# Linear attention and two mixtures of experts on one core: fewer and moved filler products, two transfers' first chunk ahead, and a reordered end of the attention

## The chip, the cores and the metric

The kernel runs on one core of a Trainium2 chip. The metric is device time of one execution in microseconds. The kernel before takes 455.93 us (median of 3 runs, 455.37 to 456.27).

## The reference

Three layers in a row, all in fp32. First a gated linear attention over 2 batches, 8 heads, 768 positions and a head width of 48; its output is the 1536 x 384 matrix x of the two layers behind it. Then a mixture of experts with one expert for each token, then one with two experts for each token and noise on the gate:

```python
for t in range(S):                                                  # attention
    state = alpha[:, :, t, :, None] * state + einsum('bhd,bhe->bhde', k[:, :, t], v[:, :, t])
    y[:, :, t] = einsum('bhd,bhde->bhe', q[:, :, t], state)
...
logits = x @ w_gate; expert_idx = argmax(logits)                    # layer 1: 8 experts, F = 1024
y = einsum('ecf,efd->ecd', maximum(einsum('ecd,edf->ecf', disp, w1), 0), w2)
...
noisy = x @ w_gate + log1p(exp(x @ w_noise)) * noise                # layer 2: the best two of 8
out[mask] += top2_w[mask, k] * (maximum(x[mask] @ w1[e], 0) @ w2[e])
```

## The kernel before

**Attention.** The 1536 positions are cut into 12 chunks of 128, numbered 0 to 11 (6 for each batch). They come into the core in five transfers, `PIECES`: (0,0), (0,2) and (0,4) with two chunks each, (1,0) and (1,3) with three; the numbers are the batch and its first chunk. (0,0) is worked on as two parts of one chunk. For each transfer `decays` (L217) makes running products of alpha on VectorE with scans (L253 to L269) and multiplies k and q by them (`times`, L243 and L244). Each of k and q has two halves in time, so there are four such multiplications for a transfer; the last two (L273, L275) complete k and q. `decays` is a generator, and each `yield` is a place where other work may be put between.

A chunk i goes through four steps. `scores` (L295): TensorE transposes k (L303), multiplies k by q (L309), ScalarE copies the results out of PSUM (L305, L317) and GpSimd zeroes the upper triangle (`affine_select`, L318). `state` (L322): the running state (L334, L336), scaled by ScalarE or VectorE (L341, L343). `mix` (L348): the output of the chunk (L356, L360, L362), copied out by ScalarE (L365). `r1_logits` (L378): the output is turned to rows and the gate's logits come with it in one product (L385); VectorE sums the logits (`gates`, L387) and ScalarE copies the rows (L394). Both read the same PSUM tile, and the one that the program names second waits for the other. `gates` comes second except for the last chunk (L390, L395).

**Routing.** Chunks are routed in groups (`GROUPS`: 0 to 2, 3 to 5, 6 and 7, 8 and 9, 10, 11). `route1` (L404) is a generator of eight steps: maximum, index and difference, one-hot row (L420), exponential on ScalarE (L422), ranks by products of ones with the one-hot rows on TensorE (L426 to L430), normalising (L432 to L435), slot numbers (L440 to L447), and the scatter of the rows to DRAM by GpSimd's indirect DMA (L158). Rows of chunks 8 to 11 (`EARLY`) aren't read back for the first expert: `first_x` (L649) takes the first 240 rows of that expert from DRAM by three transposing products (L655) and adds the four late chunks by products with one-hot columns (L662).

**Order.** The order around the change is written out by hand. `PATTERNS` has a string for each chunk i; its letters are S (`scores` of chunk i+1), T (`state`), M (`mix`), L (`r1_logits` of chunk i-1), D (a step of `decays`), R (a step of the oldest route) and W (`splits`: a piece of expert 0's weights is rounded to fp32r by ScalarE, L537, and the rest that is left goes to VectorE or GpSimd, L538). `FXR` orders what comes behind chunk 11: x is a step of `first_x`, l the logits of chunk 11, R as above. Each engine works through its own instructions in that order.

**Fillers.** `warm(n)` (L167) issues n products of a zero tile (128x512, bf16, L170) whose result nobody reads: 34 (`WARM0`) ahead of the first `scores`, 10 (`WARM2`) ahead of that of chunk 1, 20 (`FILL`) ahead of that of chunk 2, and 2 (`WARM1`) in `first_x`.

**Experts.** Behind the attention 16 experts follow (8 of each layer), each with `hidden` (L683, L686) and `second` (L714, L716 or L722), each fp32 product made of three fp32r ones. Weights come by DMA from SP's queue and are split as above. At the end the last rows go to the output by indirect DMA.

Of the kernel before, what the change touches and what calls it, by code (L numbers as in the profile page):

```python
# [12 lines left out]
ALU = mybir.AluOpType  # L13
# [17 lines left out]
P1 = C1 // T1  # L31
R = N
SPARE = E * R
WARM0 = 34
NF, ND = F // 128, DM // 128
IW = HR + E
PIECES = [(0, 0, 2), (0, 2, 2), (0, 4, 2), (1, 0, 3), (1, 3, 3)]
# [2 lines left out]
MASKS = "G" * 12  # L40
STATES = "AAAAAAAAVVVV"
DECAYS = "444444440000"
FILL = (20,)
S0 = 1
WARM1 = 2
WARM2 = 10
FXR = "xRRxRRlxRRRRRxxRxRR"
EARLY = 8
WE = "GGGGVVVVVVVVVGGG"
PATTERNS = (  # L50
    "SDDTDDM", "SDDTLDDM", "SDDTLDDM", "SDDTLRRRDDM", "SDDTLDDM", "SRRDTLRRRDDDM",
    "SDDTLRRRDDM", "WSDDTWLDDMW", "WSRRWTRRRWLRRRWMW", "RWSRWTRRRWLWMW", "STLRRRWWMW", "RRRRRLRRRM")
LATE = (0, 4)
LZ = 0
LR = (5, 6, 7, 5, 7, 8)
# [12 lines left out]
def body(tc, ap, cap, dbg=False, stop=False):  # L68
    nc = tc.nc
    V, A, G, PE = nc.vector, nc.scalar, nc.gpsimd, nc.tensor  # L70
    with ExitStack() as ctx:
# [5 lines left out]
        def sb(shape, tag, bufs, dt=F32):  # L77
            cnt[0] += 1
            return pool.tile(list(shape), dt, name=f"{tag}_{cnt[0]}", tag=tag, bufs=bufs)
# [4 lines left out]
        def s6(shape, dt=F32):  # L84
            return sb(shape, "s6", 18, dt)
# [20 lines left out]
        def pm():  # L106
            return ps("pm", 2)
# [37 lines left out]
        def load_v(b, c0, n):  # L145
            v3 = xb([128, n, DM])
            nc.sync.dma_start(v3, ap["v"][b, c0 * 128:(c0 + n) * 128].rearrange("(c p) d -> p c d", p=128))
            for c in range(n):
                vts[b, c0 + c] = v3[:, c, :]

        spacer = const([1, 1], "spacer")
        NCK = B * NC
# [14 lines left out]
        def warm(n):  # L167
            p = ph()
            for _ in range(n):
                PE.matmul(p, wt[:, :128], wt, start=True, stop=True)  # L170
# [21 lines left out]
        V.memset(att[:HR, 4 * IW + 128:], 0.0)  # L192
        warm(WARM0)
        load_v(*PIECES[0])
# [31 lines left out]
        def decays(b, c0, n):  # L226

            a6, k6, q6 = qkv[b, c0]
            w, m = n * 256, n * 4
            as_ = a6[:, 2 * w + 1:]  # L230
            key, o_, all_ = room[b, c0][:3]
            if o_ == 0:
                room[key] = (key, o_, all_, [s6([HR, all_]) for _ in range(4)])
            w6, v6, kn, qn = (x[:, o_:o_ + 2 * w] for x in room[key][3])
            w6, v6 = (x.rearrange("r (h j) -> r h j", h=2) for x in (w6, v6))
            qkv[b, c0] = (None, kn, qn)
            zv = {x: zs[x][:, :m, :] for x in zs}
            z1, z3, z4 = (zv[x].rearrange("r s j -> r (s j)") for x in ("z1", "z3", "z4"))
            w1v = w6[:, 0].rearrange("r (s j) -> r s j", j=64)
            w2v = w6[:, 1].rearrange("r (s j) -> r s j", j=64)  # L240

            def times(eng, src, dst, x, h):
                o = dst.rearrange("r (s h j) -> r s h j", h=2, j=64)[:, :, h, :]  # L243
                eng.tensor_tensor(o, src[:, h].rearrange("r (s j) -> r s j", j=64),  # L244
                                  x[:, h].rearrange("r (s j) -> r s j", j=64), op=ALU.mult)

            first, k_ = not begun, len(begun)
            z2v = z2s[k_ % 2][:, :m, :]
            z2 = z2v.rearrange("r s j -> r (s j)")
            if (b, c0) not in filled:  # L250
                V.tensor_copy(z2v[:, :, 0], as_[:, m:])
            begun.append((b, c0))
            V.tensor_tensor_scan(w6[:, 0, ::-1], a6[:, 1:w + 1][:, ::-1], z1[:, ::-1], 0.0, op0=ALU.mult, op1=ALU.add)  # L253
            times(V, k6, kn, w6, 0)
            yield
            V.tensor_tensor_scan(w6[:, 1], a6[:, w:2 * w], z2, 0.0, op0=ALU.mult, op1=ALU.add)
            if not first:
                times(V, q6, qn, w6, 1)
            yield

            whole = w1v[:, :, 0]
            ends = bass.AP(whole.tensor, whole.offset, [whole.ap[0], (w + 63, 2), (64, m)])
            z34 = zs["z3"][:, 0, 0:1]
            begins = bass.AP(z34.tensor, z34.offset, [z34.ap[0], (12 * 64 + 63, 2), (64, m)])
            V.tensor_scalar(begins, ends, SAFE, None, op0=ALU.max)
            V.reciprocal(begins, begins)
            V.tensor_tensor_scan(v6[:, 0], a6[:, 0:w], z3, 0.0, op0=ALU.mult, op1=ALU.add)
            yield
            V.tensor_tensor_scan(v6[:, 1, ::-1], a6[:, w + 1:2 * w + 1][:, ::-1], z4[:, ::-1], 0.0,  # L269
                                 op0=ALU.mult, op1=ALU.add)  # L270
            if first:
                times(V, q6, qn, w6, 1)
            times(V, k6, kn, v6, 1)  # L273
            yield
            times(V, q6, qn, v6, 0)  # L275
            if todo and todo[0][:2] in qkv:
                b2, c2, n2 = todo[0]
                filled.append((b2, c2))
                A.activation(z2s[len(begun) % 2][:, :4 * n2, 0], qkv[b2, c2][0][:, 512 * n2 + 1 + 4 * n2:], AF.Copy)

            cs = slice(c0, c0 + n)
            v4 = lambda x: x.rearrange("r (c g) -> r g c", g=4)
            V.tensor_tensor(t1s[b][:, :, cs], v4(as_[:, :m]), v4(w1v[:, :, 0]), op=ALU.mult)
            V.tensor_copy(t2s[b][:, :, cs], v4(w2v[:, :, 63]))
            lo, hi = max(c0 - 1, 0), c0 + n - 1
            if hi > lo:
                V.tensor_tensor(gts[b][:, :, lo:hi], t1s[b][:, :, lo + 1:hi + 1], t2s[b][:, :, lo:hi], op=ALU.mult)
# [91 lines left out]
        def r1_logits(j, first=True):  # L379
            js, row, l, k = grp[j]  # L380
            yT = yTs.pop(j)
            lg = pm()
            lv = lg[:, :4 * IW].rearrange("p (g n) -> p g n", g=4)
            for gp in range(4):
                PE.matmul(lv[:, gp, :], yT[:, gp, :], idw[:, gp, :], start=True, stop=True)  # L385
            def gates():
                V.tensor_reduce(l[:, k, :], lv[:, :, HR:].rearrange("p g n -> p n g"), axis=AX.X, op=ALU.add)  # L387


            if j == NCK - 1:  # L390
                gates()
            by = lambda x: x.rearrange("p (g a e) -> p g a e", g=4, a=2)
            for ab in range(2):
                A.activation(by(row[:, k, :DM])[:, :, ab, :], lv[:, :, ab * 64:ab * 64 + 48], AF.Copy)  # L394
            if j < NCK - 1:  # L395
                gates()
            if j >= EARLY and first:
                t = late[j] = sb([128, 2 * DM + C1], "b6", 5, F32R)
                A.activation(t[:, :DM], row[:, k, :DM], AF.Copy)
                G.tensor_tensor(t[:, DM:2 * DM], row[:, k, :DM], t[:, :DM].bitcast(F32), op=ALU.subtract)  # L400
            if dbg:
                nc.sync.dma_start(ap["xdbg"][j * 128:(j + 1) * 128], row[:, k, :DM])
# [247 lines left out]
        def first_x():  # L650

            at = [py()[:, :C1] for _ in range(ND)]
            for d in range(ND):
                for t in range(T1):
                    PE.matmul(at[d][:, t * P1:(t + 1) * P1], early[0][:, t, d * 128:(d + 1) * 128], ident[:P1, :P1],  # L655
                              start=(t == 0), stop=False, skip_group_check=True)
                yield
            n = N // 128
            for j in range(EARLY, n):
                for d in range(ND):  # L660
                    for i in range(2):
                        PE.matmul(at[d], late[j][:, i * DM + d * 128:i * DM + (d + 1) * 128], late[j][:, 2 * DM:],  # L662
                                  start=False, stop=(i == 1 and j == n - 1), skip_group_check=True)
                yield
            xg[0] = sb([P1, T1, RW], "b6", 5)
            nc.sync.dma_start(xg[0][:, :, DM:], xs1[:C1, DM:].rearrange("(t p) d -> p t d", p=P1))
            xh, xl = xsp[0] = (xb([128, ND, C1], F32R), xb([128, ND, C1], F32R))
            for d in range(ND):
                A.activation(xh[:, d, :], at[d], AF.Copy)
                V.tensor_tensor(xl[:, d, :], at[d], xh[:, d, :].bitcast(F32), op=ALU.subtract)  # L670
            yield
# [432 lines left out]
        for i in range(NCK):  # L1104
            left_ = int(DECAYS[i])
            for o in PATTERNS[i]:
# [15 lines left out]
                elif o == "W" and i >= SP and wi < 16:  # L1122
                    splits(wi)
                    wi += 1
            if i < len(FILL):
                warm(FILL[i])
            for fn in todo_at.get(i, ()):
# [4 lines left out]
        fx = first_x()  # L1132
        for o in FXR:
            if o == "x":
# [90 lines left out]
        for n, (layer, e) in enumerate(jobs):  # L1225
            steps = STEPS[n // E if n <= E else 2 if turned_out(n - 1) else 3]
            eng = [G if x == "G" else V for x in ENGS[layer - 1]]
# [317 lines left out]
```

## Time and profile before

| what | value |
|---|---|
| median of 3 runs | 455.93 us (455.37 to 456.27) |
| the profiled execution's own time | 457.59 us |
| its span in the profile | 456.0 us |
| PE busy | 445.1 us (98%) |
| VectorE (DVE), ScalarE (ACT), GpSimd (POOL) busy | 273.0, 266.3, 347.6 us |

The span is the time from the first to the last instruction of the profiled execution; the rest of its own time lies around it. A timeline line has a start and a duration in us, engine, line of the kernel, operation, what is written from what, and in brackets an idle time in front of it with what ended it. An end of a TensorE product is modelled and overlaps the next one, so its work is better read from starts.

### The profile page before, as it was taken

To read this page: it belongs to the slowest core of one execution; us is meant where nothing else is said; L and a number is where in the kernel's file an instruction comes from. 1 tells how busy PE (TensorE), PEld (TensorE's weight loads), DVE (VectorE), ACT (ScalarE), POOL (GpSimd) and SP (SyncE) were. 2 spreads that over 40 slices of the span, in tenths; PEclk is the share of its full clock that TensorE was granted. 3 is DMA by queue.
4 is the path that set the end of the run, shared out by engine and by line. 5 is a ranking of instruction groups with operands and counts; after the bars stand their busy time and mean duration, and the time that the engine had idled before them with its cause. 6 is when DMAs were issued, how large, how long until landed. Compare 5 with 4: busy or idle time off the path is not lost.

```text
span 456.0 us, 9516 instructions
## 1 busy us (share of the span) xinstructions
PE 445.1 (98%) x3167; PEld 418.4 (92%) x3170; DVE 273.0 (60%) x906; ACT 266.3 (58%) x703; POOL 347.6 (76%) x436
## 2 busy tenths in 40 slices
PE   8999999999999999999999999999999999999992
PEld 3688888899999999999999999999999999999992
DVE  8989986856967867878866454333443343243350
ACT  3577787467776776786651468255473464664310
POOL 3434697785998989999943379989989698799922
PEclk9999999999999999999999999999999999999997
DMA  8974972869999987876321997649287492993232
GB/s 284 407 269 150 327 260 96 259 199 313 329 307 314 269 253 224 269 226 193 123 70 55 253 324 229 136 108 323 57 262 154 129 293 57 284 246 51 27 45 43
DMA packets 73586, 93.66 MB, mean 205 GB/s; under 512 B 31962, under 2 KB 56610, under 8 KB 73526
## 3 DMA queue, kind: packets, MB, share of 16 engines
q1 hardware_dynamic: 66854, 79.98, 57.4%
q0 software_dynamic: 6672, 12.97, 12.7%
q8 instruction: 27, 0.44, 0.4%
q14 instruction: 33, 0.27, 0.2%
HBM read 70.30 MB, written 20.02 MB: 198 GB/s over the span
## 4 chain that ended last, share of the span: by engine, by line
PE 95%; DMA 1%; ACT 1%; POOL 0%; DVE 0%; issue 0%; POOLq 0%; ACTq 0%
PE ph L683 24%; PE py L722 22%; PE ph L686 12%; PE py L714 8%; PE py L716 4%; PE ph L170 4%; PE ph L309 3%; PE pm L750 3%; PE pm L385 2%; PE py L336 2%; PE py L362 2%; PE py L356 2%; DMA s<-w 1%; PE py L303 1%; PE ph L1002 1%; PE ph L975 1%
## 5 line engine op out<-in xcount | busy, mean ns | idle before, releaser
L538 POOL TENSOR_TENSOR s<-s,s 128x384 fp32r<-128x384 f32 x211 | 221.1, 1169 | 17.9 <-ACT s L537 16.3
L683 PE MATMUL ph<-x,s 128*128 128x240 f32 (+9 forms) x768 | 133.1, 308 | 0.3 <-DVE h L693 0.2
L537 ACT ACTIVATE s<-s 128x384 fp32r<-128x384 f32 x256 | 124.9, 517 | 9.5 <-DMA s<-w 7.6
L683 PEld LDWEIGHTS ph<-x,s 128*128 128x128 f32 x768 | 116.2, 189 | 1.9 <-DVE h L693 0.4
L693 DVE SCALAR_TENSOR_TENSOR h<-ph,h 128x240 fp32r<-128x240 f32 (+9 forms) x128 | 60.2, 470 | 82.8 <-ACT h L692 80.7
L692 ACT ACTIVATE h<-ph 128x240 fp32r<-128x240 f32 (+9 forms) x128 | 54.1, 423 | 75.7 <-PE ph L686 70.6
L686 PE MATMUL ph<-x,s 128*128 128x240 f32 (+9 forms) x384 | 76.2, 306 | 0.0
L158 POOL DMA_INDIRECT out<-b,m_ix x28 | 44.0, 1571 | 29.4 <-ACT b L878 9.7
L722 PE MATMUL py<-h,s 128*128 128x304 f32 (+4 forms) x360 | 65.4, 339 | 0.0
L722 PEld LDWEIGHTS py<-h,s 128*128 128x128 f32 x360 | 63.2, 188 | 0.8
L714 PE MATMUL py<-h,s 128*128 128x480 f32 (+3 forms) x192 | 61.5, 376 | 0.0
L686 PEld LDWEIGHTS ph<-x,s 128*128 128x128 f32 x384 | 60.9, 189 | 0.2
L716 PE MATMUL py<-h,s 128*128 128x240 f32 (+3 forms) x192 | 50.5, 263 | 0.0
L318 POOL TENSOR_SCALAR_AFFINE_SELECT h<-h 128x512 f32<-128x512 f32 x24 | 22.8, 975 | 30.2 <-ACT h L317 30.2
L158 POOL DMA_INDIRECT xs<-b,m_si x32 | 32.5, 1017 | 17.0 <-DVE pm L832 10.6
L722 PE MATMUL py<-s,h 128*128 128x384 f32 x216 | 38.6, 337 | 0.0
L714 PEld LDWEIGHTS py<-h,s 128*128 128x128 f32 x192 | 36.1, 188 | 2.6
L722 PEld LDWEIGHTS py<-s,h 128*128 128x128 f32 x216 | 37.8, 188 | 0.0
L716 PEld LDWEIGHTS py<-h,s 128*128 128x128 f32 x192 | 36.6, 191 | 0.0
L636 DVE TENSOR_TENSOR x<-pm,x 128x384 fp32r<-128x384 f32 (+8 forms) x42 | 19.9, 473 | 25.8 <-ACT x L635 24.8
L538 DVE TENSOR_TENSOR s<-s,s 128x384 fp32r<-128x384 f32 x45 | 30.6, 700 | 0.4 <-ACT s L537 0.2
L635 ACT ACTIVATE x<-pm 128x384 fp32r<-128x384 f32 (+8 forms) x42 | 17.7, 421 | 22.3 <-DVE pm L632 19.0
(263 smaller groups left out, 606.0 us busy)
## 6 DMA issues: line engine op xcount, KB each, us to landing
s<-w SPq DMA_DIRECT2D x28, 768.0 KB
s<-w_2b SPq DMA_DIRECT2D x22, 768.0 KB
s<-w_1b SPq DMA_DIRECT2D x14, 768.0 KB
xs<-s SPq DMA_DIRECT2D x2, 1576.0 KB
out<-s SPq DMA_DIRECT2D x4, 768.0 KB
b<-xs SPq DMA_DIRECT2D x12, 156.0 KB
b<-xs SPq DMA_DIRECT2D x12, 144.0 KB
b<-b SPq DMA_DIRECT2D x44, 36.0 KB
```

The source lines that it names most:

```text
L158: st = G.indirect_dma_start(out=dst, out_offset=bass.IndirectOffsetOnAxis(ap=ix, axis=0), in_=src, in_offset=None, **kw)
L318: G.affine_select(a_, a_, pattern=[[0, 4], [1, 128]], compare_op=ALU.is_ge, fill=0.0, base=0, channel_multiplier=-1)
L537: A.activation(hi[sl], t[sl], AF.Copy)
L538: rest.append(lambda: (eng or V).tensor_tensor(lo[sl], t[sl], hi[sl].bitcast(F32), op=ALU.subtract))
L636: rest.append(lambda: V.tensor_tensor(xl[:, d, :], y[:, :c], xh[:, d, :].bitcast(F32), op=ALU.subtract))
L683: PE.matmul(p, w, x[:, d, :], start=(k == 0), stop=False)
L686: PE.matmul(p, w1_of(n, f, d)[0], xl[:, d, :], start=False, stop=(d == ND - 1))
L692: A.activation(hh, p, AF.Relu)
L693: V.scalar_tensor_tensor(hl, p, 0.0, hh.bitcast(F32), op0=ALU.max, op1=ALU.subtract)
L714: PE.matmul(yp[o][:, :2 * c], wh[:, sl], both, start=(f == 0), stop=(f == NF - 1), skip_group_check=True)
L716: PE.matmul(yp[o][:, :c], wl[:, sl], hh, start=False, stop=(f == NF - 1), skip_group_check=True)
L722: PE.matmul(out_, l, r, start=(f == 0 and k == 0), stop=(f == NF - 1 and k == 2))
```

## The change

Five edits. `WARM0` goes from 34 to 26 and `FILL` from 20 to 23. For the transfers (0,2) and (1,3) the last two multiplications of `decays` are each cut in two, and those of the transfer's first chunk go first (k, then q), ahead of those of its other chunks. `gates` comes ahead of the copies for chunk 9 too (`FIRST`). In the string of chunk 10 `mix` goes ahead of the last three weight pieces, and in that of chunk 11 the logits of chunk 10 go ahead of the last step of the open route. In `FXR` the second step of `first_x` goes ahead of two route steps.

```diff
-WARM0 = 34
+WARM0 = 26
+FIRST = (9, 11)
+AHEAD = ((0, 2), (1, 3))
-FILL = (20,)
+FILL = (23,)
-FXR = "xRRxRRlxRRRRRxxRxRR"
+FXR = "xxRRRRlxRRRRRxxRxRR"
-    ..., "STLRRRWWMW", "RRRRRLRRRM")
+    ..., "STLRRRMWWW", "RRRRLRRRRM")
-            def times(eng, src, dst, x, h):
-                o = dst.rearrange("r (s h j) -> r s h j", h=2, j=64)[:, :, h, :]
+            def times(eng, src, dst, x, h, at=slice(None)):
+                o = dst.rearrange("r (s h j) -> r s h j", h=2, j=64)[:, at, h, :]
...
-            times(V, k6, kn, v6, 1)
-            yield
-            times(V, q6, qn, v6, 0)
+            if (b, c0) in AHEAD:
+                times(V, k6, kn, v6, 1, slice(0, 4))
+                times(V, q6, qn, v6, 0, slice(0, 4))
+                yield
+                times(V, k6, kn, v6, 1, slice(4, None))
+                times(V, q6, qn, v6, 0, slice(4, None))
+            else:
+                times(V, k6, kn, v6, 1)
+                yield
+                times(V, q6, qn, v6, 0)
...
-            if j == NCK - 1:
+            if j in FIRST:
                 gates()
...
-            if j < NCK - 1:
+            if j not in FIRST:
                 gates()
```

**VectorE, end of the decays of transfer (0,2)** (s_43 and s_44 are its running products, s_45 its k, s_46 its q). Before:

```order
L269 SCALAR_TENSOR_TENSOR s_44_293<-s_10_134,s_7_91 112x512
L244 TENSOR_TENSOR s_45_294<-s_11_135,s_44_293 112x8x64
L244 TENSOR_TENSOR s_46_295<-s_12_136,s_44_293 112x8x64
L283 TENSOR_TENSOR t_152<-s_10_134,s_43_292 112x4x2
L284 COPY t_154<-s_43_292 112x4x2
```

Now (lines of the changed kernel, L246 is L244 before):

```order
L271 SCALAR_TENSOR_TENSOR s_44_285<-s_10_126,s_7_91 112x512
L246 TENSOR_TENSOR s_45_286<-s_11_127,s_44_285 112x4x64
L246 TENSOR_TENSOR s_46_287<-s_12_128,s_44_285 112x4x64
L246 TENSOR_TENSOR s_45_286<-s_11_127,s_44_285 112x4x64
L246 TENSOR_TENSOR s_46_287<-s_12_128,s_44_285 112x4x64
L292 TENSOR_TENSOR t_144<-s_10_126,s_43_284 112x4x2
```

Two multiplications became four of half the width, and the first two complete the first chunk.

**ScalarE, chunks 10 and 11** (b_220 and s_204 belong to the rows of chunk 9, s_210 is the rounded weight pieces, m_ex the exponential of the group of chunks 8 and 9, pm_1217 the logits of chunk 10). Before:

```order
L394 ACTIVATE s_204_1077<-pm_1147 128x4x48 x2
L399 ACTIVATE b_220_1155<-s_204_1077 128x384
L537 ACTIVATE s_210_1109<-s_135_760 128x384 x2
L365 ACTIVATE h_1188<-py_1175 112x512
L537 ACTIVATE s_210_1109<-s_135_760 128x384
L422 ACTIVATE m_ex_1161<-m_lm_1160 128x16
L394 ACTIVATE s_233_1214<-pm_1217 128x4x48 x2
```

Now (L374 is L365 before, L546 is L537, L431 is L422, L403 is L394):

```order
L403 ACTIVATE s_204_1076<-pm_1146 128x4x48 x2
L408 ACTIVATE b_220_1154<-s_204_1076 128x384
L374 ACTIVATE h_1183<-py_1170 112x512
L546 ACTIVATE s_210_1108<-s_135_758 128x384 x3
L431 ACTIVATE m_ex_1160<-m_lm_1159 128x16
L403 ACTIVATE s_233_1209<-pm_1212 128x4x48 x2
```

The output of `mix` is copied ahead of the three pieces, and all three pieces now stand between it and the exponential.

**TensorE, behind chunk 11** (py_1254, py_1255 and py_1256 are the three accumulators of `first_x`, pm_1260 the ranks of chunk 10, pm_1279 the logits of chunk 11). Before:

```order
L655 MATMUL py_1254<-iw_83,b_203_1073 128x120 x2
L426 MATMUL pm_1260<-eb_185,ones 128x8
...
L427 MATMUL pm_1260<-acc_189,ones 128x8
...
L430 MATMUL pm_1260<-m_oh_1233,tri 128x8
L655 MATMUL py_1255<-iw_83,b_203_1073 128x120 x2
L385 MATMUL pm_1279<-s_4_80,h_1252 128x120 x4
```

Now (L664 is L655 before, L435 to L439 are L426 to L430, L394 is L385):

```order
L664 MATMUL py_1253<-iw_83,b_203_1072 128x120 x2
L664 MATMUL py_1254<-iw_83,b_203_1072 128x120 x2
...
L435 MATMUL pm_1261<-eb_177,ones 128x8
...
L436 MATMUL pm_1261<-acc_181,ones 128x8
...
L439 MATMUL pm_1261<-m_oh_1232,tri 128x8
L394 MATMUL pm_1278<-s_4_80,h_1251 128x120 x4
```

The second transposing product went ahead of the ranks of chunk 10.

## Rows read from the trace of the kernel before

**Rows 1.** The page, part 1: busy time, share of span, instructions.

```profile
PE 445.1 (98%) x3167; PEld 418.4 (92%) x3170; DVE 273.0 (60%) x906; ACT 266.3 (58%) x703; POOL 347.6 (76%) x436
```

**Rows 2.** Busy by engine in the attention; behind POOL: granted clock, DMA share, GB/s.

```profile
0.00:90.00 90.00, 87.96 (x843) 68.87 (x846) 77.91 (x206) 59.18 (x175) 53.88 (x85) 1.00 0.74 258
```

**Rows 3.** The chain that ended last: by engine; two pieces (start, us, what).

```profile
PE 95%; DMA 1%; ACT 1%; POOL 0%; DVE 0%; issue 0%; POOLq 0%; ACTq 0%
...
220.18 0.67 PE ph L683 x6
220.93 6.27 DMA s<-w
```

**Rows 4.** Timeline of PE: fillers, and the first products of `scores` 0, 1, 2, 9.

```profile
1.52 10.29 PE L170 MATMUL ph<-warm 128*128 128x512 bf16 x34 [1.52 <-POOL warm L165]
11.65 0.55 PE L303 MATMUL py<-iw,s 112*128 112x112 f32 x4
...
15.39 0.55 PE L303 MATMUL py<-iw,s 112*128 112x112 f32 x4
...
18.94 4.49 PE L170 MATMUL ph<-warm 128*128 128x512 bf16 x19
23.26 0.55 PE L303 MATMUL py<-iw,s 112*128 112x112 f32 x4
...
61.78 0.60 PE L303 MATMUL py<-iw,s 112*128 112x112 f32 x4
```

**Rows 5.** Timeline of DVE: the multiplications, two equal scans, an idle time.

```profile
7.41 1.07 DVE L244 TENSOR_TENSOR s<-s,s 112x256 f32<-112x256 f32 x3
...
12.41 0.76 DVE L244 TENSOR_TENSOR s<-s,s 112x256 f32<-112x256 f32 x2
...
15.48 1.65 DVE L256 TENSOR_TENSOR_SCAN s<-s,s 112x512 f32<-112x512 f32 x1
...
21.18 1.30 DVE L244 TENSOR_TENSOR s<-s,s 112x512 f32<-112x512 f32 x2
...
24.61 1.22 DVE L256 TENSOR_TENSOR_SCAN s<-s,z 112x512 f32<-112x512 f32 x1
...
28.71 0.19 DVE L387 TENSOR_REDUCE m_l<-pm 128x8 f32<-128x32 f32 x1 [1.91 <-ACT s L394]
...
58.82 2.51 DVE L244 TENSOR_TENSOR s<-s,s 112x768 f32<-112x768 f32 x2
```

**Rows 6.** Timeline of POOL: the first two selects.

```profile
13.99 2.06 POOL L318 TENSOR_SCALAR_AFFINE_SELECT h<-h 128x512 f32<-128x512 f32 x2 [8.48 <-ACT h L317]
```

**Rows 7.** Timeline of PE, end of the attention.

```profile
80.06 0.18 PE L426 MATMUL pm<-eb,ones 1*128 1x16 bf16 x1
...
80.89 1.15 PE L385 MATMUL pm<-s,h 112*128 112x120 f32 x8 [0.20 <-ACT h L365]
...
84.61 0.18 PE L427 MATMUL pm<-acc,ones 128*128 128x8 bf16 x1
84.71 0.17 PE L430 MATMUL pm<-m_oh,tri 128*128 128x8 bf16 x1
84.73 0.68 PE L655 MATMUL py<-iw,b 120*128 120x120 f32 x4
85.25 1.06 PE L385 MATMUL pm<-s,h 112*128 112x120 f32 x8
```

**Rows 8.** Timeline of ACT, end of the attention.

```profile
79.29 0.92 ACT L537 ACTIVATE s<-s 128x384 fp32r<-128x384 f32 x2
80.25 0.60 ACT L365 ACTIVATE h<-py 112x512 f32<-112x512 f32 x1
...
81.15 0.21 ACT L422 ACTIVATE m_ex<-m_lm 128x16 f32<-128x16 f32 x1
```

**Rows 9.** Timeline of DVE, end of the attention.

```profile
81.65 0.15 DVE L432 TENSOR_REDUCE m_se<-m_ex 128x2 f32<-128x16 f32 x1
...
83.79 0.19 DVE L387 TENSOR_REDUCE m_l<-pm 128x8 f32<-128x32 f32 x1
...
84.50 0.16 DVE L420 TENSOR_TENSOR m_oh<-io,m_j 128x8 bf16<-128x8 f32 x1
```

More of the change, by code (lines that the diff above doesn't have):

```diff
@@ L51 @@
     "SDDTDDM", "SDDTLDDM", "SDDTLDDM", "SDDTLRRRDDM", "SDDTLDDM", "SRRDTLRRRDDDM",
-    "SDDTLRRRDDM", "WSDDTWLDDMW", "WSRRWTRRRWLRRRWMW", "RWSRWTRRRWLWMW", "STLRRRWWMW", "RRRRRLRRRM")
+    "SDDTLRRRDDM", "WSDDTWLDDMW", "WSRRWTRRRWLRRRWMW", "RWSRWTRRRWLWMW", "STLRRRMWWW", "RRRRLRRRRM")
 LATE = (0, 4)
@@ L240, in decays @@
             w2v = w6[:, 1].rearrange("r (s j) -> r s j", j=64)
-            def times(eng, src, dst, x, h):
-                o = dst.rearrange("r (s h j) -> r s h j", h=2, j=64)[:, :, h, :]
-                eng.tensor_tensor(o, src[:, h].rearrange("r (s j) -> r s j", j=64),
-                                  x[:, h].rearrange("r (s j) -> r s j", j=64), op=ALU.mult)
+            def times(eng, src, dst, x, h, at=slice(None)):
+                o = dst.rearrange("r (s h j) -> r s h j", h=2, j=64)[:, at, h, :]
+                eng.tensor_tensor(o, src[:, h].rearrange("r (s j) -> r s j", j=64)[:, at],
+                                  x[:, h].rearrange("r (s j) -> r s j", j=64)[:, at], op=ALU.mult)
             first, k_ = not begun, len(begun)
```

## The prediction

> **What bounds the kernel now.** I read the page's busy times first: TensorE is busy for 445.1 of 456.0 us [rows 1]. The chain that ended last says the same in another way: 95% of it is TensorE's own work [rows 3]. So what counts is TensorE's queue: a product taken out of it is worth its duration as long as nothing behind it has to wait. Then the windows: in the attention (0 to 90 us) TensorE is busy for 87.96 us at a granted clock of 1.00, the 2.4 GHz level [rows 2]. But part of that is fillers, whose result nobody reads, so the question for the front is what the real work behind each group of fillers was waiting for. TensorE's timeline gives the starts of that work [rows 4], VectorE's the time at which its operands were ready [rows 5].
>
> **Fillers.** The 20 fillers between chunks 0 and 1 begin at 18.94 and `scores` of chunk 2 at 23.26: 4.32 / 20 = 0.216 us each (the row counts 19; a record is missing) [rows 4]. The first 34 begin at 1.52 and end at 11.65: 10.13 / 34 = 0.298 us each. The price of the eight that go is therefore between 0.216 and 0.298 us. I take 0.216, since those left out are in effect the last ones of the group, and every filler behind them has that price, while the dear ones must be the first of the group. That saves 8 x 0.216 = 1.73 us (2.38 at the other end). The three that are added cost 3 x 0.216 = 0.65 us. Net: -1.08 us (-1.73 at the other end). The granted clock shows 1.00 over the whole stretch and so doesn't show the dear part.
>
> The Trainium skill has the reason for the two prices: "TensorE: Matmul & The Clock Gate", Part 1, says that the array starts at half rate and that a product of 512 columns is then issued every 426.7 ns, against 215.7 ns at full rate. By the second figure, an estimate from that page, the sum would be the same -1.08 us; by the first it would be eight times 0.427 less three times 0.216, -2.77 us.
>
> **Is the work ready when it moves?** Three places.
>
> `scores` of chunk 0 would start at 11.65 - 1.73 = 9.92. Its k and q are complete when the three multiplications from 7.41 end, at 8.48 [rows 5]. It doesn't wait.
>
> `scores` of chunk 1 moves from 15.39 to 13.66 [rows 4], its products with q some 0.5 us behind its transposes, to 14.1. Its k and q are complete at 12.41 + 0.76 = 13.17 [rows 5]. Margin 0.5 us for k and 0.9 for q.
>
> `scores` of chunk 2 moves from 23.26 to 23.26 - 1.08 = 22.18, and its products with q to 22.7. Before, the two wide multiplications end at 21.18 + 1.30 = 22.48 [rows 5]; k is there at 21.8, q at 22.5, so q would be late or nearly so if anything slipped. Now the first chunk takes two of 256 elements, 0.76 us for two by the row at 12.41, and is complete at 21.94, 0.2 us ahead of the transposes and 0.7 ahead of the products. So the cut pays for the smaller number of fillers here; by itself it gives nothing. Its cost is at most 4 x 0.38 - 1.30 = 0.22 us on VectorE, and VectorE idles 1.91 us soon after, until ScalarE has copied the rows of chunk 0 [rows 5]. That idle time goes with TensorE's work, since the logits come from it, so VectorE's later work moves forward with TensorE's. I cost the cut at nothing; without that cover it would be 0.2 us.
>
> The other transfer that is cut, (1,3): its two multiplications end at 58.82 + 2.51 = 61.33, `scores` of chunk 9 starts at 61.78 [rows 4, 5]. It isn't waiting, and both move by the same 1.08. I cost this at nothing too. That k's buffer is let go one or two multiplications later (up to 0.8 us by halves of that row) delays the SP queue's next weight load; the queue then runs later, but I find no wait of TensorE on it in the chain of this stage.
>
> **The end of the attention.** TensorE starts the ranks of chunks 8 and 9 at 80.06 and then waits for the copied output of `mix` 10, until 80.89 [rows 7]. That copy is issued at 80.25, behind two weight pieces that end at 80.21 [rows 8]. With `mix` ahead of the pieces it can start when the last product of `mix` is done, which is near 80.06 to 80.13. Gain 0.12 to 0.19 us; I take 0.15. `gates` of chunk 9 ahead of its copies makes the one-hot rows earlier by up to the two copies; the ranks then end earlier, but the product behind them waits for the copy just named: nothing.
>
> The other side of the same move: three pieces (0.46 us each by the row at 79.29) now stand between the copy and the exponential. It was at 81.15; it will be near 80.1 + 0.6 + 3 x 0.46 = 82.1. VectorE reads it at once (before: at 81.65, behind other work) and everything behind that on VectorE waits, up to the logits of chunk 10 at 83.79 and their one-hot row at 84.50 to 84.66 [rows 9]. If that chain starts at 82.2 instead of 81.65, the one-hot row comes near 85.2. Before, TensorE's ranks of chunk 10 needed it at 84.71 and waited a little (0.10 us from 84.61, where the next step is 0.02) [rows 7]. Now the second transposing product goes first, 0.52 us by 84.73 to 85.25, and with the 0.15 gained the ranks come to 84.61 + 0.52 - 0.15 = 84.98. They wait some 0.2 us where they waited 0.1. Bounds: nothing, if VectorE finds less to wait for beside GpSimd, and 0.7 us, if its two steps behind the exponential are held up by GpSimd's work. I take +0.1. GpSimd's queue gets the low part of chunk 10's rows ahead of the scatter of chunks 8 and 9; in that stretch it idles for DVE anyway, cost nothing. The end together: -0.15 + 0.1 = -0.05, between -0.2 and +0.6.
>
> **Behind it.** The experts are TensorE's own work. The one transfer on the chain, 6.27 us from 220.93, starts when a product of `hidden` ends (220.18 + 0.67) [rows 3]: it moves with TensorE. So a gain ahead of 90 us should come through.
>
> **The sum.** -1.08 - 0.05 = -1.13 us. Against the profiled execution: 457.59 - 1.13 = 456.46 us (span 454.9). The median of the runs is 1.66 us lower than that execution, so the forecast is 455.93 - 1.13 = **454.8 us**.
>
> **The rivals.**
>
> *A: the end eats half of it.* The exponential is late by 0.95 us, VectorE's chain behind it by as much plus what GpSimd holds up, and the ranks of chunk 10, the logits of chunk 11 and all behind them move by up to 0.6 us. For it: everything behind the exponential is in order on one engine. Against it: VectorE had 0.5 us between exponential and use. Time: 455.93 - 1.08 + 0.6 = 455.4. Chance 0.2.
>
> *B: `scores` of chunk 1 or 2 waits.* The first two selects on GpSimd (2.06 us from 13.99) move to 12.3, right beside the multiplications of chunk 1's k and q [rows 5, 6]. Beside them before, a scan took 1.65 us, where its equal at 24.61 took 1.22. If the multiplications lose 0.43 us each, q is complete at 14.0, just in time. If each is held for one whole select (1.03 us), k comes at 13.8 and q at 15.2, and TensorE waits for 1.1 us: 455.93 - 1.08 + 1.1 - 0.05 = 455.9. The same time results if the cut of transfer (0,2) doesn't do what it says, because `scores` 2 waits for all four multiplications: at most 0.5 us, 455.3. Chance 0.1.
>
> The Trainium skill speaks for B: "SBUF — State Buffer", in its glossary and its section on who contends, says that VectorE with two SBUF inputs and GpSimd share a port pair that one instruction holds to its end while the other fully blocks. The slower scan agrees in kind; its 0.43 us is less than one select, so the trace shows a part of that price only.
>
> *C: slower, by the clock.* Eight fillers fewer end the opening group at 9.92. If TensorE then sits waiting long enough for its clock to fall, the work behind it runs at the price of the start again: the opening group cost 10.13 - 34 x 0.216 = 2.79 us more than at the later price [rows 4]. The point from which it decides is a real wait between fillers and `scores`, in B's places. Then 455.93 - 1.13 + 2.79 = 457.6. For it: fewer fillers. Against it: the margins above, and a granted clock of 1.00 throughout [rows 2]. Chance 0.05.
>
> *D: more.* The eight cost 0.298 each: 455.93 - 1.73 - 0.05 = 454.15. Chance 0.05.
>
> **How the numbers follow.** The forecast has the remaining 0.6, with some 0.4 us around it for the unknown end (-0.2 to +0.6 instead of -0.05) and for the medians, whose runs lie 0.9 us apart. The range from 453.8 to 455.9 takes in D, A and most of B; C and what is left at the edges are left out. About 0.2% (0.91 us) is what a measurement of this kernel can tell from no change, so faster means under 455.02. That holds for most of the forecast (0.55 of its 0.6) and D: 0.6. A, B and the rest of the forecast are within it: 0.34. C and a bad draw: 0.06.
>
> **What would show it.** In the profile after: `scores` of chunk 0 near 9.9, of chunk 2 near 22.2 without idle time ahead, the first expert's first product 1.1 us earlier than its 90 us now, and TensorE's work unchanged behind it. The exponential of chunks 8 and 9 should lie some 0.9 us later against TensorE, and the ranks of chunk 10 should show what that costs. I am wrong if TensorE idles or its products stretch at chunks 1 or 2, or if the 1.1 us are there at 30 us and gone at 90.

## The result and the profile after

The changed kernel is slower. Its median is 459.64 us (458.39 to 460.2, 6 runs) against 456.1 us of the kernel before beside it (455.37 to 457.32, 6 runs): ratio 1.0072, 95% interval 1.0052 to 1.0091. The forecast was 454.8 us, with a range of 453.8 to 455.9. On a second chip, in an experiment below, the ratio was 1.0108 (1.0091 to 1.0125).

In the changed kernel the lines stand 2 to 9 further down than in the kernel before: the multiplications of `times` are L246 (L244 before), the transposes of `scores` L312 (L303), the selects L327 (L318), the copy of `mix` L374 (L365), the logits L394 (L385), `gates` L396 (L387), the difference and the one-hot row L427 and L429 (L418, L420), the exponential L431 (L422), the ranks L435 to L439 (L426 to L430), the weight pieces L546 and L547 (L537, L538), the first expert's products L692 (L683).

The page of the changed kernel, head and two rows. The busy time of TensorE is 1.7 us less than in [rows 1] and the span is 2.1 us longer, so idle time was added. The row of the granted clock has an 8 among its nines.

```profile
span 458.1 us, 9509 instructions
...
PE 443.4 (97%) x3162; PEld 418.8 (91%) x3165; DVE 272.9 (60%) x910; ACT 268.1 (59%) x703; POOL 348.4 (76%) x436
...
PEclk9999989999999999999999999999999999999997
```

TensorE's timeline of the changed kernel (start, us, engine, line, what, idle time ahead and what ended it):

```profile
1.52 7.25 PE L172 MATMUL ph<-warm 128*128 128x512 bf16 x26 [1.52 <-POOL warm L167]
8.61 0.55 PE L312 MATMUL py<-iw,s 112*128 112x112 f32 x4
...
13.61 0.60 PE L312 MATMUL py<-iw,s 112*128 112x112 f32 x4 [1.10 <-DVE s L246]
...
22.18 0.55 PE L312 MATMUL py<-iw,s 112*128 112x112 f32 x4
...
60.70 0.60 PE L312 MATMUL py<-iw,s 112*128 112x112 f32 x4
...
63.38 0.17 PE L435 MATMUL pm<-eb,ones 1*128 1x24 bf16 x1 [0.99 <-DVE m_l L396]
...
64.83 0.19 PE L438 MATMUL pm<-m_oh,ones 128*128 128x16 bf16 x2 [1.16 <-DVE m_oh L429]
...
66.60 1.95 PE L394 MATMUL pm<-s,h 112*128 112x120 f32 x8
...
70.84 0.60 PE L312 MATMUL py<-iw,s 112*128 112x112 f32 x4
...
83.65 1.15 PE L394 MATMUL pm<-s,h 112*128 112x120 f32 x8 [0.49 <-ACT h L374]
...
88.73 0.17 PE L439 MATMUL pm<-m_oh,tri 128*128 128x8 bf16 x1 [0.62 <-DVE m_oh L429]
```

Against [rows 4], `scores` of chunk 2 is at 22.18 and of chunk 9 at 60.70, both 1.08 us earlier, as forecast to the hundredth. That is luck: `scores` of chunk 0 starts 3.04 us earlier (8.61 instead of 11.65) and not 1.73, and chunk 1 then waits 1.10 us for VectorE, where the forecast had no wait. Then chunk 9 takes 10.14 us to `scores` of chunk 10 (60.70 to 70.84), where the kernel before takes 6.25 (61.78 to 68.03). Of these 3.89 us, 0.99 + 1.16 = 2.15 are two waits for VectorE, and the rest are products that stretch behind them: the logits at 66.60 take 1.95 us. The first expert starts at 93.84, 3.58 us later than before (90.26). In the kernel before the same products stood like this, without a wait:

```profile
63.41 0.18 PE L426 MATMUL pm<-eb,ones 1*128 1x24 bf16 x1
...
63.65 0.19 PE L429 MATMUL pm<-m_oh,ones 128*128 128x16 bf16 x2
...
65.13 1.08 PE L385 MATMUL pm<-s,h 112*128 112x120 f32 x8
```

What VectorE and GpSimd do ahead of the two waits, first in the kernel before, then in the changed one (timelines of DVE and of POOL):

```profile
58.82 2.51 DVE L244 TENSOR_TENSOR s<-s,s 112x768 f32<-112x768 f32 x2
61.26 0.60 DVE L283 TENSOR_TENSOR t<-s,s 112x12 f32<-112x12 f32 x1
...
61.98 0.49 DVE L287 TENSOR_TENSOR gt<-t,t 112x12 f32<-112x12 f32 x1
62.39 0.18 DVE L387 TENSOR_REDUCE m_l<-pm 128x8 f32<-128x32 f32 x1
...
63.38 0.21 DVE L420 TENSOR_TENSOR m_oh<-io,m_j 128x24 bf16<-128x24 f32 x1
```

```profile
57.93 4.52 POOL L318 TENSOR_SCALAR_AFFINE_SELECT h<-h 128x512 f32<-128x512 f32 x4
62.42 1.00 POOL L538 TENSOR_TENSOR s<-s,s 128x384 fp32r<-128x384 f32 x1
```

```profile
57.73 3.51 DVE L246 TENSOR_TENSOR s<-s,s 112x256 f32<-112x256 f32 x4
61.17 0.97 DVE L292 TENSOR_TENSOR t<-s,s 112x12 f32<-112x12 f32 x1
...
62.31 0.92 DVE L296 TENSOR_TENSOR gt<-t,t 112x12 f32<-112x12 f32 x1
63.15 0.18 DVE L396 TENSOR_REDUCE m_l<-pm 128x8 f32<-128x32 f32 x1
...
64.11 0.66 DVE L429 TENSOR_TENSOR m_oh<-io,m_j 128x24 bf16<-128x24 f32 x1
```

```profile
56.85 3.86 POOL L327 TENSOR_SCALAR_AFFINE_SELECT h<-h 128x512 f32<-128x512 f32 x4
60.68 1.43 POOL L547 TENSOR_TENSOR s<-s,s 128x384 fp32r<-128x384 f32 x1
...
62.21 1.93 POOL L547 TENSOR_TENSOR s<-s,s 128x384 fp32r<-128x384 f32 x2
```

The two multiplications of 768 elements took 2.51 us; cut into two of 256 and two of 512 they take 3.51, for the same elements. GpSimd's four selects go the other way, from 4.52 to 3.86. The tiny operations behind them (12 and 24 elements) then lie beside GpSimd's multiplications and take 0.97, 0.92 and 0.66 us, where they took 0.60, 0.49 and 0.21. So `gates` starts 0.76 us later, at 63.15 instead of 62.39, and 1.84 us later against TensorE, which is 1.08 ahead.

### The profile page after: what moved, and what is told of

Same layout as the page of the kernel before. It is cut to its first block, busy times and chain, and to the rows that moved or that the text cites. A ratio compares the mean times of both kernels' runs of the same rounds, so it can differ in the third digit from the quotient of the medians.

```text
span 458.1 us, 9509 instructions
## 1 busy us (share of the span) xinstructions
PE 443.4 (97%) x3162; PEld 418.8 (91%) x3165; DVE 272.9 (60%) x910; ACT 268.1 (59%) x703; POOL 348.4 (76%) x436
## 4 chain that ended last, share of the span: by engine, by line
PE 91%; DVE 3%; ACT 1%; DMA 1%; issue 1%; POOL 0%; POOLq 0%; ACTq 0%; DVEq 0%
PE ph L692 24%; PE py L731 22%; PE ph L695 12%; PE py L723 8%; PE py L725 4%; PE pm L759 3%; PE pm L394 2%; PE ph L318 2%; PE py L345 2%; PE py L365 2%; PE py L371 2%; DMA s<-w 1%; PE ph L172 1%; PE py L312 1%; PE ph L1011 1%; PE ph L984 1%
## 5 line engine op out<-in xcount | busy, mean ns | idle before, releaser
L547 POOL TENSOR_TENSOR s<-s,s 128x384 fp32r<-128x384 f32 x211 | 220.8, 1165 | 17.3 <-ACT s L546 15.8
L692 PE MATMUL ph<-x,s 128*128 128x240 f32 (+9 forms) x768 | 132.6, 308 | 0.0
L546 ACT ACTIVATE s<-s 128x384 fp32r<-128x384 f32 x256 | 124.4, 516 | 11.9 <-DMA s<-w 9.1
L692 PEld LDWEIGHTS ph<-x,s 128*128 128x128 f32 x768 | 116.2, 189 | 0.9 <-ACT x L678 0.2
L327 POOL TENSOR_SCALAR_AFFINE_SELECT h<-h 128x512 f32<-128x512 f32 x24 | 23.9, 1018 | 27.0 <-ACT h L326 27.0
L547 DVE TENSOR_TENSOR s<-s,s 128x384 fp32r<-128x384 f32 x45 | 28.1, 643 | 1.2 <-ACT s L546 0.9
```

Source lines behind the costliest of these rows:

```text
L327: G.affine_select(a_, a_, pattern=[[0, 4], [1, 128]], compare_op=ALU.is_ge, fill=0.0, base=0, channel_multiplier=-1)
L546: A.activation(hi[sl], t[sl], AF.Copy)
L547: rest.append(lambda: (eng or V).tensor_tensor(lo[sl], t[sl], hi[sl].bitcast(F32), op=ALU.subtract))
L692: PE.matmul(p, w, x[:, d, :], start=(k == 0), stop=False)
```

## The experiments

Letters in the expectations: theory S is that the second cut, (1,3), makes VectorE late because GpSimd's work holds its shorter pieces; the other theories put the loss on the smaller number of fillers (F), on the reordered end (E), or on a price that short multiplications have by themselves (P).

**One part at a time.** e1 is the changed kernel without the second cut:

```diff
-AHEAD = ((0, 2), (1, 3))
+AHEAD = ((0, 2),)
```

> The changed kernel with the two multiplications of transfer (1,3) whole again; all other edits stay. Theory S (the cut of (1,3) does the harm: four short multiplications on VectorE are held up by GpSimd's selects more often than two long ones, so the gates and the one-hot rows of chunks 3 to 5 come late, TensorE waits twice in chunk 9 and its clock falls): the two waits of 1.0 and 1.2 us go, the granted clock in the 60 to 70 us window is 1.00, the transposes of chunk 10 start near 66.9 us, 1.1 us ahead of the kernel before; what is left over the forecast is the end, +0.7: 455.7 us. Rival F (the fillers' shift alone sets VectorE and GpSimd against each other): the waits stay, 459 us. Rival E (the reordered end costs it): the waits in chunk 9 may go, but the time stays above 458.

e2 is the kernel before with that cut and nothing else (`times` and the branch on `AHEAD` as in the change):

```diff
+FIRST = (11,)
+AHEAD = ((1, 3),)
```

> The kernel before with the cut of (1,3) alone. Theory S: TensorE waits some 2.1 us in chunk 9 and loses 1.7 us at the lower clock, as in the changed kernel, so the transposes of chunk 10 are 3.9 us later than before (68.0 to 71.9) and the time is 457.5 to 460, nearer to 459. Rival F: like the kernel before, 456.1. Rival E: 456.1.

e3 is the kernel before with the fillers and the first cut:

```diff
-WARM0 = 34
+WARM0 = 26
+AHEAD = ((0, 2),)
-FILL = (20,)
+FILL = (23,)
```

> The kernel before with the fillers moved (26 and 23) and the cut of (0,2) alone. Theory S: TensorE is 1.08 us ahead from chunk 2 to the first expert, 455.0 us. Rival F: two waits in chunk 9, 459 us. Rival E: 455.0.

e4 is the kernel before with the reordered end (`FIRST`, `FXR` and `PATTERNS` of the change).

> The kernel before with the end reordered alone (gates of chunk 9 first, mix of chunk 10 ahead of the last weight pieces, the logits and the second step of the first expert's rows moved). Theory S, with what the trace of the changed kernel shows of the end: the copied output of chunk 10 is no earlier than 0.1 us, the exponential behind three weight pieces makes the ranks of chunk 10 wait some 0.6 us, so the first expert starts 0.5 to 0.8 us later: 456.1 + 0.6 = 456.7 us. Rival E: over 458 us. Rival F: 456.1 to 456.7.

Measured, with the kernel before at 457.21 us on that chip:

| kernel | median us | ratio to before | 95% interval | span us |
|---|---|---|---|---|
| e1, without the second cut | 457.26 | 1.0001 | 0.9983 to 1.0018 | 455.0 |
| e2, second cut alone | 460.45 | 1.0082 | 1.0054 to 1.0110 | 458.2 |
| e3, front alone | 457.14 | 1.0003 | 0.9985 to 1.0021 | 455.3 |
| e4, end alone | 457.56 | 1.0016 | 0.9997 to 1.0034 | 455.4 |

The second cut alone makes all of the loss, and without it nothing is lost. In e2's trace the same two waits stand at TensorE:

```profile
64.05 0.17 PE L435 MATMUL pm<-eb,ones 1*128 1x24 bf16 x1 [1.00 <-DVE m_l L396]
...
65.49 0.19 PE L438 MATMUL pm<-m_oh,ones 128*128 128x16 bf16 x2 [1.16 <-DVE m_oh L429]
```

But e1, e3 and e4 aren't faster either, so the gain that I forecast is missing too. That is the second question, below.

**Is it GpSimd, or the shortness?** e5 is the changed kernel without the selects of chunks 7 and 8, e6 the same without the second cut:

```diff
                 A.activation(a_.rearrange("p a b -> p (a b)"), s_, AF.Copy)
+                if i in (7, 8):
+                    continue
                 G.affine_select(a_, a_, ...
```

> The changed kernel without GpSimd's four selects of chunks 7 and 8, so the upper triangles of these two chunks' scores stay in and the outputs of these chunks are other numbers. Both cuts stay. Theory S (GpSimd holds VectorE's instructions, and each further piece is one more hand-over): the four multiplications of the cut transfer are near what they take without neighbour, two of 256 at 0.38 and two of 512 near 0.67, 2.1 us in all instead of 3.51; the gates and the one-hot rows are on time, TensorE has none of its two waits of 0.99 and 1.16 us, scores 10 starts 6.2 to 6.4 us behind scores 9 (10.14 in the changed kernel), and the time is about that without the second cut, 457 to 457.5 on this chip. Rival P (short multiplications are dear by themselves): they still take near 3.5 us, and the time stays above 460.

> The same without the second cut: four selects of chunks 7 and 8 left out (outputs of these chunks are other numbers), cut only for the first transfer. Theory S: the two multiplications of 768 take near 0.96 us each, 1.9 in all, where they took 2.51 beside the selects; time within 0.5 us of the kernel with both cuts and no selects, so that the cut's price goes from 3.5 us to under 0.5. Rival P: this one is faster than that by about 3 us.

e5 took 455.83 us, ratio 0.9997 (0.9986 to 1.0008); e6 455.81 us, 0.9998 (0.9987 to 1.0009). The cut's price went from 3.2 us (e2 against before: 460.45 - 457.21) to nothing measurable in the time. The rows on the multiplications show why (the view of one line: count, then ns of the shortest, the middle and the longest); in order: the kernel before, the changed kernel, e5, e6.

```profile
L244 DVE TENSOR_TENSOR s<-s,s x2: 1206/1294/1381, 58.8 to 60.0; 112x768 f32<-112x768 f32 x2
```

```profile
L246 DVE TENSOR_TENSOR s<-s,s x4: 670/980/1116, 57.7 to 60.1; 112x256 f32<-112x256 f32 x2, 112x512 f32<-112x512 f32 x2
```

```profile
L246 DVE TENSOR_TENSOR s<-s,s x4: 417/555/684, 58.5 to 59.8; 112x256 f32<-112x256 f32 x2, 112x512 f32<-112x512 f32 x2
```

```profile
L246 DVE TENSOR_TENSOR s<-s,s x2: 951/954/958, 57.9 to 58.7; 112x768 f32<-112x768 f32 x2
```

Without the selects beside them the four take 1.96 us together and the two 1.83: cutting by itself costs 0.13. Beside the selects each instruction of VectorE takes longer, and four are held four times: 3.51 - 1.96 = 1.55 us against 2.51 - 1.83 = 0.68 for two. Taken one by one, the first in a row loses 0.25 us and each further one 0.42 or 0.43, whether it has 256, 512 or 768 elements. The durations beside the selects are the same to 0.01 us in all five profiles with the second cut and in all eight without it. Theory S stands, P falls. e5 kept one wait of 0.47 us for the one-hot row, since the tiny operations (0.98 and 0.92 us) still lay beside GpSimd's weight pieces; its chunk 9 took 6.77 us, where e6's took 6.16.

**The stretched products.** Windows of the changed kernel (stretch; sum; busy time of PE, PEld, DVE, ACT, POOL with counts; granted clock, DMA share, GB/s):

```profile
62.00:64.00 2.00, 0.68 (x10) 0.41 (x7) 1.97 (x14) 1.65 (x4) 2.00 (x4) 1.00 0.90 336
64.00:66.00 2.00, 1.17 (x12) 0.87 (x12) 0.88 (x3) 1.05 (x3) 2.00 (x4) 0.99 1.06 401
66.00:68.00 2.00, 2.00 (x12) 2.00 (x12) 1.06 (x4) 0.00 (x0) 0.32 (x2) 0.50 1.03 383
68.00:70.00 2.00, 2.00 (x15) 1.87 (x16) 1.91 (x16) 0.96 (x3) 1.09 (x3) 0.65 0.09 29
```

The clock that was granted falls to 0.50, the 1.2 GHz level, after 2.15 us of idling in 4. e2 had the same waits and kept its clock in its profile, so its chunk 9 took 8.52 us instead of 10.14. e7 puts fillers where TensorE idled, so that the waits cost the same but TensorE stays busy:

```diff
-    ... "WSRRWTRRRWLRRRWMW", ...
+    ... "WSFRRWTRRRWLRRRWMW", ...
+                elif o == "F":
+                    warm(11)
```

> The changed kernel with 11 fillers (2.4 us at 0.216) between the products of scores 9 and the ranks, where TensorE had idled for 2.15 us. If the lower granted clock behind the waits is a part of the loss in the time, the granted clock stays at 1.00 through 60 to 72 us, scores 10 starts near 69.2 instead of 70.84, and the time falls by up to 1.6 us, to 458.5 to 459. If the loss is the wait alone (the kernel with the late cut alone had the same wait, no lower clock and the same time), the time stays within 0.5 us of the changed kernel's, 460.4 on this chip.

e7: 459.01 us, ratio 1.0069 (1.0050 to 1.0088), on another chip than the changed kernel's 1.0072. Its profile had `scores` of chunk 10 at 69.15, as expected for a kept clock, but the time told nothing. So both were run again on one chip, where the kernel before took 457.49 us:

> The changed kernel once more, on the same chip as the same kernel with 11 fillers in its wait. If the granted clock usually falls behind the two waits (mean clock 0.989 to 0.993 in four of the first five runs with it), the profile shows 0.5 to 0.65 in 66 to 70 us again and scores 10 about 10.1 us behind scores 9; the time is 0.72% over the kernel before.

> 11 fillers in the wait, once more, on the same chip as the changed kernel. If the fall of the clock belongs to the loss, this one is 0.8 to 1.7 us faster than the changed kernel beside it; if the loss is the wait alone, the two are within 0.5 us. The first pair, on two chips, gave 1.0072 and 1.0069 of the kernel before, each by some 0.002.

The changed kernel: 462.49 us, 1.0108 (1.0091 to 1.0125). With the fillers: 459.53 us, 1.0047 (1.0032 to 1.0063). One of the windows, of the changed kernel again (e12) and with fillers (e13):

```profile
66.00:68.00 2.00, 2.00 (x12) 2.00 (x12) 0.51 (x2) 0.00 (x0) 0.36 (x2) 0.50 1.06 391
```

```profile
66.00:68.00 2.00, 2.00 (x21) 2.00 (x20) 1.20 (x6) 0.40 (x2) 0.42 (x2) 1.00 1.04 385
```

So the loss has two parts: the wait itself, some 2.0 us (459.53 - 457.49), and the clock behind it, which costs 1.46 to 1.62 us in the profiles where it fell (10.10 and 10.14 us for chunk 9, against 8.64 and 8.63 with fillers and 8.52 in e2) and 3.0 in the medians of that chip (462.49 - 459.53). Useless work in the wait gave back more than half of the loss there. That the medians differ by more than the profiles isn't explained. The profiled run of e12 is its fastest, with a mean granted clock of 0.991, and the four others have 0.986 to 0.989; a longer stretch at the lower clock would fit, but no profile shows one. The ends of the two intervals that lie nearest to each other (1.0091 and 1.0063) would leave 1.3 us.

The mean granted clock of every run, profiled or not, says that e2's profile is the exception. It is 0.992 or lower in 14 of the 18 runs of the kernels whose profiles show both waits without fillers in them (4 of 6 of the changed kernel, 5 of 7 of e2, 5 of 5 of e12), in 1 of the 12 of e7 and e13, and in 1 of the 87 runs of the kernel before beside the experiments. In e2 the two runs at 0.995 took 459.88 and 459.96 us, and the five others 460.31 to 462.68.

**Where did the 1.08 us go?** e8 has the fillers of the change and no cut at all (`WARM0` 26, `FILL` 23). e10 and e11 are the kernel before, unchanged, for further profiles of it.

> The kernel before with 26 and 23 fillers and no cut at all. If the cut of the first transfer pays for the smaller number of fillers, as I predicted, scores 2 or its products with q wait for the second wide multiplication here, by 0.2 to 0.5 us, and chunk 2 and all behind it are that much later than in the kernel with cut and fillers (22.1); if the cut gives nothing, scores 2 starts at 22.1 to 22.2 too. Time within 0.3% of the kernel before either way, 456.5 to 457.5.

> The kernel before once more, for a second profile of it. If the length of the dear part of the opening fillers changes from execution to execution (in the seven profiles so far the fillers of 0.36 us each last until 4.3 to 6.5 us), scores 0 starts anywhere from 10.2 to 11.7, and scores 9 from 61.1 to 61.8. If VectorE's last one-hot row is usually held by GpSimd in the old end (1.15 us with the late cut alone, with the front alone and with the fillers alone, 0.20 in the profile shown), the last ranks wait 0.7 us here and the first expert starts 29.4 us behind scores 9; otherwise 28.5 as in the profile shown.

> The kernel before a third time, for the same question: scores 0 between 10.2 and 11.7, the last ranks with a wait of 0.7 us or without one.

e8: 456.31 us, ratio 1.0003 (0.9994 to 1.0011). `scores` of chunk 2 starts at 22.28 without a wait and chunk 3 at 28.20, 5.92 us later, where the changed kernel has 5.80: so the first cut gives 0.1 us, not 0.2 to 0.5. e10 and e11 took 457.41 and 455.67 us in their one execution. What the opening group costs isn't fixed. The view of the fillers' line, in two stretches of the profile that I predicted from and in one of e11 (shortest, middle and longest ns; first and last start):

```profile
L170 PE MATMUL ph<-warm x6: 634/634/634, 3.6 to 5.8; 128*128 128x512 bf16 x6
L170 PE MATMUL ph<-warm x8: 379/416/634, 5.8 to 8.0; 128*128 128x512 bf16 x8
```

```profile
L170 PE MATMUL ph<-warm x9: 379/379/634, 3.6 to 5.9; 128*128 128x512 bf16 x9
```

The fillers of 634 ns are the dear ones (six from 1.5 to 3.6, 0.42 us from start to start; the cheap ones of the middle value 379 stand 0.216 apart, as in [rows 4]; the 0.36 in the expectation of e10 was misread). In the profile shown they last beyond 5.8 us, in e11 they end between 3.6 and 5.9. With 34 fillers `scores` of chunk 0 is at 11.65, 11.80, 11.22, 10.39 and 10.21 in the five profiles (before, e10, e2, e11, e4), and `scores` of chunk 9 at 61.78, 61.93, 61.35, 61.03 and 61.10. With 26 it is at 60.52 to 60.91 in nine of ten profiles and at 61.18 in e5. In e11 TensorE already waits for VectorE at chunk 2:

```profile
22.40 0.57 PE L303 MATMUL py<-iw,s 112*128 112x112 f32 x4 [0.23 <-DVE s L244]
```

So the smaller number of fillers saves 1.1 us when the dear part is long, and some 0.3 when it is short, because there VectorE sets the start of chunks 1 and 2. In the changed kernel chunk 1 starts at 13.61 behind 1.10 us of waiting: the two scans ahead of its multiplications took 1.03 and 1.05 us beside GpSimd's first selects, where they took 0.69 and 0.66 in the kernel before. By the means of these profiles (61.44 and 60.76) it saves 0.7.

The profile shown had the opposite luck at the end. TensorE's last ranks wait for a one-hot row of 8 elements. In the profile shown VectorE starts it at 87.83, with a GpSimd addition from 87.95, and it takes 0.20 us (DVE, then POOL):

```profile
87.83 0.20 DVE L420 TENSOR_TENSOR m_oh<-io,m_j 128x8 bf16<-128x8 f32 x1
```

```profile
87.95 1.01 POOL L400 TENSOR_TENSOR b<-s,b 128x384 fp32r<-128x384 f32 x1
```

In e10, e11, e2, e3 and e8 the two starts lie in the same order, 0.13 or 0.14 us apart, and the row takes 1.15 us, to the end of the addition. What decides between the two isn't shown. Here it is in e10 (DVE, then POOL, then PE):

```profile
87.90 1.15 DVE L420 TENSOR_TENSOR m_oh<-io,m_j 128x8 bf16<-128x8 f32 x1
```

```profile
88.04 0.98 POOL L400 TENSOR_TENSOR b<-s,b 128x384 fp32r<-128x384 f32 x1
```

```profile
89.10 0.17 PE L430 MATMUL pm<-m_oh,tri 128*128 128x8 bf16 x1 [0.69 <-DVE m_oh L420]
```

From `scores` of chunk 10 to the first expert it is 22.23 us in the profile shown, and 23.01, 23.01, 23.22, 23.20 and 23.22 in those five. The new end takes 22.99 to 23.00 in e1, e4, e7 and e13 and in both profiles of the changed kernel. So against these five the end of the change costs nothing and gives at most 0.2 us, and e4's ratio can't be told from 1.

**The exponential first.** e9 is e1 with the exponential of chunks 8 and 9 ahead of `mix` and of the three pieces:

```diff
-    "STLRRRMWWW", "RRRRLRRRRM")
+    "STLRRRRMWWW", "RRRLRRRRM")
```

> The changed kernel without the second cut, and with the exponential of chunks 8 and 9 issued ahead of mix 10's copy and of the three weight pieces, where the changed kernel has it behind them. If the late exponential causes the 0.62 us wait of TensorE at the ranks of chunk 10 (88.73 in the changed kernel, 84.86 without the second cut), VectorE's chain behind the exponential starts 0.9 us earlier, that wait goes, and the first expert starts 0.4 to 0.6 us earlier against scores 9 than without this move (89.96 - 60.73 = 29.2 us there, so 28.6 to 28.8). Rival: mix 10's copy is pushed back by the exponential (0.2 us) and the ranks' wait goes to the copy; first expert as before, 29.2. The time: at most 0.13% less than the kernel before's, which 5 rounds can hardly tell.

e9: 455.35 us, ratio 0.9985 (0.9972 to 0.9997), against 455.97 for the kernel before beside it. It is the only version whose interval lies below 1. The exponential and the first expert (ACT, PE):

```profile
78.30 0.20 ACT L431 ACTIVATE m_ex<-m_lm 128x16 f32<-128x16 f32 x1
79.03 0.60 ACT L374 ACTIVATE h<-py 112x512 f32<-112x512 f32 x1 [0.53 <-PE py L371]
```

```profile
88.99 1.01 PE L692 MATMUL ph<-x,s 128*128 128x240 f32 x6
```

There is no wait left at the ranks of chunk 10. From `scores` of chunk 9 to the first expert it takes 88.99 - 60.63 = 28.36 us against 29.23 in e1, 0.87 less and more than the 0.4 to 0.6 expected; the copy of `mix` 10 isn't pushed back, since the exponential fits ahead of its operands (79.03, with 0.53 us of idling).

## Why the prediction was wrong

**The step that failed** is the second cut: "It isn't waiting, and both move by the same 1.08. I cost this at nothing too." I looked at the one consumer that the cut is for, `scores` of chunk 9, which indeed doesn't wait. I priced the buffer that is let go later, but not two more instructions on VectorE beside GpSimd's selects, and did not look at what is queued behind them on VectorE: `gates` and the one-hot row. The trace of before shows how little room these had. `gates` is done at 62.39 + 0.18 = 62.57 and the ranks begin at 63.41, a margin of 0.84; the one-hot row is done at 63.38 + 0.21 = 63.59 and its product begins at 63.65, a margin of 0.06 us. Anything longer on VectorE had to become a wait. Measured: 1.0 us more for the multiplications, 0.8 for the two tiny operations behind, 0.45 for the one-hot row; from that two waits of 2.15 us together; and 1.5 to 1.6 us of slower clock in two of the three profiles that had these waits without fillers in them.

**The rule stood in my rivals, at the wrong place.** For chunks 1 and 2 I weighed that VectorE could be held by GpSimd for whole instructions; there the multiplications lost little (1.43 us for the four of the first cut, 1.30 for the two before, [rows 5]), but the two scans ahead of those of chunk 1 lost 0.73 us. TensorE's wait of 1.10 us there was a sign that I had named for being wrong, and the sum hid it. At chunk 9, where four selects in a row lie beside them, the same thing decides. The Trainium skill, "SBUF — State Buffer", section "SBUF: two separate sides", says that a VectorE instruction with two SBUF inputs and a GpSimd instruction that reads SBUF exclude each other for a whole instruction. The trace agrees for the one-hot row of 8 elements, which took 1.15 us, to the end of an addition of 0.98, in five profiles and 0.20 in the sixth. The multiplications lost less than a whole select (two selects took 1.21 us by themselves): 0.39 us each as four (1.55) and 0.34 each as two (0.68). So the price goes by the number of instructions, not by their elements.

**Fillers.** The sum of -1.08 came out to the hundredth in the profile by two errors that cancel, 3.04 us saved at chunk 0 instead of 1.73 and a wait of 1.10 us at chunk 1 instead of none, and it was mis-sized for the time. I took one execution's opening (10.13 us) as the price; in five executions 34 fillers end from 10.21 to 11.80. My case C had the dear part as a risk behind the fillers; it is instead a part of varying length inside them, and in executions where it is short VectorE sets the start. Measured in the time: nothing, at most 0.3 us (e8: 0.9994 at the lower end). Of the 0.7 us that the profiles show at `scores` of chunk 9, 0.2 may go at the old end (23.2 us in e3 and e8, 23.0 in e10 and e11; but e2, with 34 fillers, has 23.2 too). Where the rest goes isn't shown. The Trainium skill, "TensorE: Matmul & The Clock Gate", Part 1, says that the number of slow products at the start changes from run to run; the rows above agree, and I used that page for the two prices and not for this.

**The end.** Forecast -0.05 with +0.1 for the ranks of chunk 10. They wait 0.62 us (88.73) where they had waited 0.1, as rival A has it, for VectorE stands idle for 2.33 us until the exponential is done:

```profile
84.73 0.20 ACT L431 ACTIVATE m_ex<-m_lm 128x16 f32<-128x16 f32 x1
```

```profile
84.97 0.17 DVE L441 TENSOR_REDUCE m_se<-m_ex 128x2 f32<-128x16 f32 x1 [2.33 <-ACT m_ex L431]
```

The other half I missed: in the new order the last one-hot row no longer meets GpSimd's addition, which takes the usual wait of 0.69 us away. The two cancel. The 0.15 us for the copy of `mix` 10 did not come: the ranks' follower waits 0.49 us for it, 0.20 before.

**The rivals.** Slower by the clock (rival C, 0.05) has the mechanism of the second part of the loss, at another place and behind another wait than I named: not between fillers and `scores`, but at the ranks 60 us later. Behind the attention the loss came through only in part in the profile shown (3.58 us at the first expert, 2.1 in the span), mostly since the profile of before took 1.15 us longer than the changed kernel's for the stretch from 178.73 to 213.33 (34.60 us against 33.45). e10 and e11 took 33.43 and 33.44 there, so this belongs to the execution and not to the change.

## What to carry to other kernels

Where VectorE and GpSimd both work on SBUF, count instructions, not elements: here each multiplication beside GpSimd's selects cost 0.25 to 0.43 us more, however narrow, and a tiny operation could cost a whole GpSimd addition (1.15 us instead of 0.16 to 0.20). For each instruction that is added to an engine, follow its queue to the next thing that the bounding engine waits for, and work out that margin, also when the added instruction's own consumer is fine. And before an opening's price or a margin of 0.1 us goes into a sum, take a second profile of the same kernel: here two executions of the same kernel differ by 1.4 us in the first 12 us (e10 and e11), and by 0.8 at the end (the profile shown and e10).

## What the runs showed of the hardware that I had not expected

- The opening's dear fillers end between 3.6 and 5.9 us in one execution and after 5.8 us in another, while the granted clock shows 1.00 throughout.
- Two waits of 0.99 and 1.16 us, with 0.3 us of small products between, were followed by a granted clock of 0.50 in two profiles and by 1.00 in a third (e2, 66 to 68 us), which by the mean clocks above is the rarer outcome:

```profile
66.00:68.00 2.00, 2.00 (x22) 1.89 (x19) 0.78 (x3) 0.00 (x0) 0.99 (x2) 1.00 1.05 388
```

- Cutting VectorE's multiplications made GpSimd's selects faster (4.52 to 3.86 us for four), so GpSimd reached its next work 1.74 us earlier (60.68 instead of 62.42; 1.08 of it is the earlier start of the whole stretch) and held VectorE there.
